# Attention, dense feed-forward and routed experts in one launch: conversions spread out, the opening reordered, scatters and evacuations regrouped

## The chip, the cores and the metric

The kernel runs on one core of a Trainium2 chip. The metric is the device time of one execution in microseconds (us), as the median of several runs. TensorE does the matmuls (PE, with its weight loads as PEld), VectorE is DVE, ScalarE is ACT, GpSimd is POOL, and SyncE (SP) issues most of the DMAs. Each engine works through its own instructions in the order in which the kernel writes them.

## What is computed

The program chains three blocks. The first is bucketed attention over 2 batches x 8 heads, 768 positions, head size 64: a query only sees keys with the same six sign bits of a random projection, and a row without any match falls back on the mean of all values. The second is a dense feed-forward block with a 2048-wide hidden layer and a relu6 gate, on 1536 tokens of width 512. The third routes each token to the best two of eight experts (noisy gate), each expert being a 512-1024-512 block, and adds the two weighted results.

```python
attn = softmax(where(q_bucket == k_bucket, q @ k.T / 8, -1e9)); x = attn @ v
h = x @ w_in;  x = (h * clip(h + 3, 0, 6) / 6) @ w_out
n = x @ w_gate + log1p(exp(x @ w_noise)) * noise
out = sum over the top two e of n:  softmax2(n)[e] * (relu(x @ w1[e]) @ w2[e])
```

The dense weights arrive as 64-bit floats, so the kernel converts them to 32-bit floats on the chip, in 32 halves of a 128x1024 block, and writes them to a scratch tensor `w32` in HBM, from where the dense block loads them.

## The kernel before, in words

**Attention** (line 282 on) runs over 8 pairs of heads (p), each with two halves of the queries (a half of a pair is called hb, 16 in all) and six key tiles, so 96 steps g; a pair is 12 steps (j = 0 to 11). One step does, on TensorE, the four score matmuls of the next step (`scores`, lines 476 and 477; the second of them needs the rows that `stab2` has put into tile A), two matmuls of the running row maximum two halves ahead (`maxes`, line 439, with its reduction on VectorE in line 443), and at every odd g the 48 small matmuls of attention times values for two steps (`av`, line 490). ScalarE makes the exponentials (line 478).

Around it, on GpSimd and VectorE: `stab` (lines 453 to 456, GpSimd) turns the maxima of a finished half into the rows that are transposed and sent into A (`stab2`, lines 464 to 467, the send is a small DMA of ScalarE); `uniform` (line 342, GpSimd) makes the fallback; `finish` (lines 502 to 510) adds it on VectorE, takes the reciprocal and multiplies on GpSimd into `x_all`; `lows` (line 360, GpSimd) makes the low halves of a later pair; `load_v` (line 319) loads the values two pairs ahead, at j = 2, and writes a column of ones on GpSimd (line 320); `v_sum` (lines 326 to 328, GpSimd, five additions, j = 6) sums the values over the key tiles; `bits`, `bits_all` and `move_mask` compute the sign bits and copy them by DMA into the operand tiles A and B.

**The conversion** `conv` (lines 189 to 211) is a generator, resumed once per step by `conv_step`: load 512 KB, wait, two passes on ScalarE (200, 201) and one on VectorE (202), one more on VectorE (205) and an addition on GpSimd (206), then VectorE again (208), then the store. In attention its three tiles come from the pools of the dense weights (three raw buffers `wr`, three high parts `wh`, three low parts `wl`). A conversion starts at every g with g % 3 == 1 until NU = 24 have started; the other eight start at every second step of the dense block. The weights of the first three dense steps are loaded at g = 84 to 86 into the same raw buffers, and split (`w_hi` on ScalarE, `w_lo` on VectorE, line 235) for the first two of them at g = 88 to 91.

**The opening** (lines 525 to 606) prepares the first pair without waiting for the bulk path: constants on VectorE, memsets of the operand tiles on GpSimd, the masks of pair 0 by copies (`mask_q`, line 556, on VectorE) and those of pair 1 by DMA. `bit_consts` (lines 111 to 113), twelve small copies on VectorE, is run with step 0.

**The dense block** takes 48 steps u: three chunks of 512 tokens times 16 hidden tiles, in two passes that are parted at hidden tile FSPLIT = 6. Each step has 12 matmuls into the hidden tile (line 257), activation and split on ScalarE and VectorE, and 12 matmuls into the output (lines 701 to 703). When a chunk is complete, `routing` runs as a generator beside the following steps: transposes, gate, top two, positions (`rt_pos`, lines 807 to 828), and eight indirect scatters of GpSimd into the expert buffers `xg` (`rt_scatter`, line 839). The last chunk's routing runs beside the first expert part, as the table ROUTE says.

**The experts** come in ten parts of eight steps v (`PARTS`); the first two take 224 tokens that the first two chunks filled. `e_load` (line 889) reads a part from `xg`, `e_meta` (898 to 903) its token numbers and weights, `e_out` (973 to 976) scales the result and adds it into the output by an indirect DMA of GpSimd. The part that is loaded third, the first that needs the last chunk's tokens, is loaded through GpSimd's queue.

## Time and profile before

| | us |
|---|---|
| median of 3 runs (917.21 to 921.72) | 918.85 |
| the profiled execution | 919.49 |
| its span, first to last instruction | 917.8 |
| TensorE busy (x6313 matmuls) | 848.0, 92% |
| VectorE, ScalarE, GpSimd busy | 513.6, 423.1, 244.9 |

The span is what the views divide up; 1.7 us of the execution lie outside it. A view of stretches gives each engine's busy time in a stretch, the TensorE clock that was granted there (1.00 is 2.4 GHz, 0.5 is 1.2 GHz, and a mean between says which part of the stretch had which), and the share of the time in which the DMA engines were busy. A matmul's busy time at the lower level is longer, so a busy TensorE is not a fast one. "[7.62 <-DMA V]" behind an instruction means that its engine stood idle for 7.62 us before it and that the named one ended the idle time.

### The profile page before, as it was taken

What the parts mean: (1) busy time and instruction counts of PE and PEld (TensorE: products, weight loads), DVE (VectorE), ACT (ScalarE), POOL (GpSimd) and SP (SyncE); (2) the same over time, 40 slices, a digit from 0 to 9 for tenths busy, and PEclk for the clock granted to TensorE, in tenths of its full rate; (3) what the DMA queues carried; (4) which work ended last, traced back from release to release, by engine and by line L of the source; (5) the groups of instructions that cost most, each with busy time, mean ns of one, the idle gap of its engine ahead of it and who ended that gap; (6) DMA issues with size and microseconds to landing.
All of it is one profiled execution on the core that took longest, in us unless ns stands there. A gap on an engine that the chain in (4) does not pass through costs nothing. (4 is left out here: it accounts for less than half of the span.)

```text
span 917.8 us, 15981 instructions
## 1 busy us (share of the span) xinstructions
PE 848.0 (92%) x6313; PEld 734.3 (80%) x6313; DVE 513.6 (56%) x859; ACT 423.1 (46%) x712; POOL 244.9 (27%) x286
## 2 busy tenths in 40 slices
PE   5889977787899999999999999889999999999993
PEld 2677766676788888888888888769999999999982
DVE  8657856565634666544665566645545445545561
ACT  4356544354555566544444444434433443443551
POOL 9166555274432121100012031521020120202211
PEclk8889998798999999999999999999999999999997
DMA  7655864945603459872225245696465666546671
GB/s 246 164 152 182 262 185 135 260 132 173 190 27 116 160 190 311 281 242 93 92 84 192 70 162 177 209 239 164 140 151 158 144 151 157 136 140 140 177 207 20
DMA packets 52347, 151.74 MB, mean 165 GB/s; under 512 B 8741, under 2 KB 9661, under 8 KB 52265
## 3 DMA queue, kind: packets, MB, share of 16 engines
q1 hardware_dynamic: 44393, 131.02, 46.6%
q0 software_dynamic: 7648, 19.53, 9.4%
q8 instruction: 51, 0.84, 0.4%
q14 instruction: 31, 0.25, 0.1%
q10 hardware_dynamic: 224, 0.10, 0.0%
HBM read 105.89 MB, written 32.41 MB: 151 GB/s over the span
## 5 line engine op out<-in xcount | busy, mean ns | idle before, releaser
L235 DVE TENSOR_TENSOR wl<-wr,wh 128x1024 fp32r<-128x1024 f32 (+1 forms) x128 | 155.9, 1218 | 126.2 <-ACT wh L229 126.2
L229 ACT CAST wh<-wr 128x1024 fp32r<-128x1024 f32 x128 | 134.4, 1050 | 120.0 <-PE S L946 75.8
L478 ACT ACTIVATE E<-S 128x384 f32<-128x384 f32 x192 | 90.5, 490 | 107.6 <-PE S L477 102.4
L976 POOL DMA_INDIRECT out_dram<-ot,ti x28 | 43.8, 1563 | 233.8 <-ACT ot L975 185.4
L443 DVE TENSOR_REDUCE mc<-mx 128x1 f32<-128x768 f32 x96 | 90.6, 951 | 19.7 <-PE mx L439 19.5
L439 PE MATMUL mx<-B,A 128*128 128x384 f32 x192 | 70.9, 383 | 27.3 <-DVE mc L443 24.9
L490 PEld LDWEIGHTS o<-V,E 128*64 128x64 f32 x2304 | 80.0, 151 | 13.8 <-issue 12.2
L273 DVE SCALAR_TENSOR_TENSOR g<-t,mx 128x512 f32<-128x512 f32 x47 | 32.4, 689 | 102.9 <-ACT t L272 102.9
L490 PE MATMUL o<-V,E 128*64 128x66 f32 x2304 | 86.8, 238 | 0.0
L701 PE MATMUL S<-wh,gh 128*128 128x512 f32 (+1 forms) x208 | 82.5, 397 | 0.0
L703 PE MATMUL S<-wh,gl 128*128 128x512 f32 (+1 forms) x208 | 81.6, 392 | 0.0
L702 PE MATMUL S<-wl,gh 128*128 128x512 f32 (+1 forms) x208 | 81.5, 392 | 0.0
L476 PE MATMUL S<-QX,KS 128*128 128x384 f32 x192 | 77.6, 404 | 2.5 <-ACT E L478 2.4
L477 PE MATMUL S<-A,B 128*128 128x384 f32 x192 | 68.8, 358 | 7.3 <-DMA A<-mr 7.3
L944 PE MATMUL S<-hh,wh 128*128 128x416 f32 x192 | 70.6, 368 | 0.0
L945 PE MATMUL S<-hh,wl 128*128 128x416 f32 x192 | 67.5, 352 | 0.0
L946 PE MATMUL S<-hl,wh 128*128 128x416 f32 x192 | 67.4, 351 | 0.0
L439 PEld LDWEIGHTS mx<-B,A 128*128 128x128 f32 x192 | 39.1, 208 | 34.6 <-DVE mc L443 30.6
L925 ACT ACTIVATE hh<-mx 128x416 fp32r<-128x416 f32 (+2 forms) x72 | 33.0, 459 | 65.6 <-PE mx L257 65.6
L272 ACT ACTIVATE t<-mx,half 128x512 f32<-128x512 f32 x47 | 32.3, 688 | 66.2 <-PE mx L257 66.2
L257 PE MATMUL mx<-xh,wh 128*128 128x512 f32 (+1 forms) x252 | 62.2, 369 | 0.6 <-ACT wh L229 0.6
L257 PE MATMUL mx<-xh,wl 128*128 128x512 f32 (+1 forms) x252 | 60.5, 362 | 0.6 <-DVE wl L235 0.6
(246 smaller groups left out, 1640.4 us busy)
## 6 DMA issues: line engine op xcount, KB each, us to landing
wr<-in_we_dram SPq DMA_DIRECT2D x80, 512.0 KB
wr<-w SPq DMA_DIRECT2D x48, 512.0 KB
c_raw<-in_wm_dram SPq DMA_DIRECT2D x32, 512.0 KB
xg<-pt SPq DMA_DIRECT2D x8, 838.5 KB
raw<-in_kq_dram SPq DMA_DIRECT2D x8, 768.0 KB
w<-c_ta SPq DMA_DIRECT2D x24, 256.0 KB
B<-in_kq_dram POOLq DMA_DIRECT2D x7, 768.0 KB, 8.2
xr<-xg SPq DMA_DIRECT2D x5, 838.5 KB
```

Of the source, the lines that this page charges most:

```text
L229: nc.scalar.copy(hi, W[k][0])
L235: nc.vector.tensor_tensor(lo[:, :n], W[k][0][:, :n], W[k][1][:, :n].bitcast(F32), op=ALU.subtract)
L257: nc.tensor.matmul(h, a[:, d * 128:(d + 1) * 128], b[:, d], start=i == 0 and d == 0, stop=i == 2 and d == 3)
L439: nc.tensor.matmul(pm[:, hf, :QW], t["A"][:, qh, q0:q0 + 128], t["B"][:, h, hf * QW:(hf + 1) * QW], start=True, stop=True)
L443: nc.vector.tensor_reduce(t["mc"][:, c:c + 1], pm[:, :, :QW], axis=AX.XY, op=ALU.max)
L476: nc.tensor.matmul(s[:, :QW], t["KS"][:, h, ks], t["QX"][:, qh, qs], start=True, stop=False)
L478: nc.scalar.activation(E[g % NE][:, h], s[:, :QW], ACTF.Exp, scale=0.125)
L490: nc.tensor.matmul(t["av"][r:r + 64, c:c + VW], E[g % NE][:, h, i * 128 + r:i * 128 + r + 64], t["V"][:, kt, h], start=kt == 0 and h == 0 ...
L701: nc.tensor.matmul(o, gh[:, ts], wh, start=first, stop=False)
L702: nc.tensor.matmul(o, gh[:, ts], wl, start=False, stop=False)
L703: nc.tensor.matmul(o, gl[:, ts], wh, start=False, stop=last)
L944: nc.tensor.matmul(o, wh[:, ds], hh, start=ft == 0, stop=False)
```

## The change

Conversions in attention start every sixth step (g % 6 == 3) until 16 have started, instead of every third until 24, and each has two more steps between GpSimd's addition and VectorE's last pass; the other 16 start in three of four dense steps. The ones column is written, and the values summed, at j = 8 instead of j = 2 and 6, and the sum is one reduction of VectorE. GpSimd's product of `finish` moves to the end of the next step. In the opening, `bit_consts` goes to the constants, two pairs of memsets move back and become one each, the second half of pair 0's masks is copied by ScalarE, the first scores come four matmuls into the second half's maxima, and pair 1's mask bits come behind pair 0's maxima, `stab`, `stab2` and `low_q(0)`. FSPLIT becomes 7. The routing generator does its last two transposes in one go and has no pause behind its last scatter; by ROUTE the last chunk's four scatter calls then come together in step v = 3, where the last of them stood behind the part's output scatters. `e_meta(0)` goes from v = 1 to v = 5. The output tiles of the small parts are computed and evacuated one by one.

```diff
-NU = 24
+NU = 16
-ROUTE = [(4, 0, 0), (1, 1, 0), (0, 1, 0), (4, 0, 0)]
+ROUTE = [(3, 0, 0), (1, 1, 0), (0, 1, 0), (5, 0, 0)]
-FSPLIT = 6
+FSPLIT = 7
...
+    bit_consts()
...
         nc.gpsimd.tensor_tensor(t, t, r, op=ALU.add)
-        yield
+        for _ in range(3 if fine else 1):
+            yield
         nc.vector.scalar_tensor_tensor(a, u, 2.0 ** -15, t.bitcast(F32), op0=ALU.is_ge, op1=ALU.mult)
...
-            nc.gpsimd.memset(t["V"][:, :, :, 64:], 1.0)
...
+        def v_sum(p, fill=True):
+            t = T[p]
+            if fill:
+                nc.gpsimd.memset(t["V"][:, :, :, 64:], 1.0)
             vr = sm_p.tile([128, 2 * VW], F32, name="vr")
-            nc.gpsimd.tensor_tensor(vr, V[:, 0], V[:, 1], op=ALU.add)
-            for k in range(2, KT):
-                nc.gpsimd.tensor_tensor(vr, vr, V[:, k], op=ALU.add)
+            nc.vector.tensor_reduce(vr, t["V"].rearrange("p k h c -> p (h c) k"), axis=AX.X, op=ALU.add)
...
-                finish(p, qh, t["av"])
+                at(g + 1, finish(p, qh, t["av"]))
...
-            nc.gpsimd.tensor_tensor(x, ov[:, :, :, 0:64],
-                                    r.unsqueeze(3).to_broadcast([128, 2, KT // 2, 64]), op=ALU.mult)
+            return lambda: nc.gpsimd.tensor_tensor(
+                x, ov[:, :, :, 0:64], r.unsqueeze(3).to_broadcast([128, 2, KT // 2, 64]), op=ALU.mult)
...
-            nc.vector.tensor_copy(A[64:96, hf, h * QW:(h + 1) * QW], mb[64 + 32 * h:96 + 32 * h, hf].bitcast(F32))
+            f = nc.scalar.copy if hf else nc.vector.tensor_copy
+            f(A[64:96, hf, h * QW:(h + 1) * QW], mb[64 + 32 * h:96 + 32 * h, hf].bitcast(F32))
...
-        v_sum(0)
+        nc.gpsimd.memset(T[0]["V"][:, :, :, 64:], 1.0)
+        first_k()
+        mask_q(1, 0)
+        mask_q(1, 1)
+        for i in range(NI):
+            maxes(*more(1, 1)[0])
...
         stab(0)
+        stab2(0)
+        low_q(0)
         for hf in range(2):
             T[1]["pb"] = pbs[hf]
             bits2(1, hf)
             bits3(1, hf)
             lows(1, hf)
...
+        nc.gpsimd.memset(AT[1][64:128].bitcast(F32), 0.0)
+        nc.gpsimd.memset(AT[2][64:128].bitcast(F32), 0.0)
...
-            if i == 5:
+            if i == 3:
+                for _ in scores(0):
+                    pass
+            elif i == 7:
                 low_q(1)
-        for _ in scores(0):
-            pass
+        v_sum(0, False)
...
-            if p + 1 < NP and j == 6:
+            if p + 1 < NP and j == 8:
                 v_sum(p + 1)
-                at(g + 5, v_sum2, p + 1)
+                at(g + 3, v_sum2, p + 1)
...
-                conv_step(1 if g % 3 == 1 and cvn[0] < NU else 0, None, True)
+                conv_step(1 if g % 6 == 3 and cvn[0] < NU else 0, None, True)
...
         for d in range(4):
-            yield rt_trans(c, d)
+            rt_trans(c, d)
+            if d != 2:
+                yield
...
             rt_scatter(c, t)
-            yield
+            if t < 3:
+                yield
...
+            for t in range(nt):
+                gemm2(y, NMU + v, hh, hl, n // nt, ft == 0, ft == 7, (t,))
+                if ft == 7:
+                    e_out(q, t, y[0][:, t, :])
...
-        conv_step(1 - u % 2, cvm_p, False)
+        conv_step(1 if u % 4 < 3 else 0, cvm_p, False)
...
-        if v == 1:
+        if v == 5:
             e_meta(0)
```

## Rows read from the trace of the kernel before

**Rows 1.** Stretches: engines' busy time (instructions), granted clock, DMA share, GB/s; attention by pairs.
```profile
0.00:26.50 26.50, 15.43 (x67) 7.72 (x68) 21.69 (x40) 10.15 (x13) 22.20 (x30) 0.78 0.75 242
26.50:62.20 35.70, 29.56 (x343) 24.46 (x344) 19.68 (x39) 16.11 (x34) 13.06 (x20) 0.83 0.47 128
62.20:88.25 26.05, 25.55 (x380) 21.07 (x376) 20.80 (x31) 16.97 (x37) 16.83 (x30) 1.00 0.78 232
88.25:118.98 30.73, 27.60 (x387) 22.79 (x388) 22.17 (x32) 16.97 (x37) 18.41 (x26) 0.94 0.69 206
118.98:155.48 36.50, 29.52 (x386) 24.29 (x384) 22.27 (x32) 16.86 (x37) 18.34 (x26) 0.86 0.63 191
155.48:193.03 37.55, 29.44 (x386) 24.13 (x384) 22.37 (x32) 16.84 (x37) 18.39 (x26) 0.86 0.63 185
193.03:230.37 37.34, 29.59 (x386) 24.29 (x384) 21.36 (x32) 16.89 (x37) 18.36 (x26) 0.86 0.58 165
230.37:260.00 29.63, 26.89 (x373) 23.24 (x370) 18.93 (x29) 14.45 (x33) 13.44 (x23) 0.94 0.57 166
260.00:286.00 26.00, 25.08 (x404) 20.58 (x402) 7.37 (x12) 13.74 (x30) 5.98 (x8) 1.00 0.12 42
286.00:556.00 270.00, 270.00 (x1242) 222.25 (x1237) 152.78 (x267) 134.43 (x188) 33.63 (x30) 1.00 0.51 170
556.00:626.00 70.00, 63.05 (x393) 53.84 (x392) 44.05 (x106) 32.41 (x57) 19.91 (x16) 0.95 0.71 206
```

**Rows 2.** Waits of TensorE from 62.2 to 260 us: total us, times, longest.
```profile
PE mx L439 <- DVE mc L443: 20.7, 10, 3.3
PE S L477 <- DMA A<-mr: 7.3, 5, 2.5
```

**Rows 3.** Waits of VectorE and of GpSimd in the same stretch.
```profile
DVE c_ta L208 <- POOL c_ta L206: 57.9, 22, 6.6
...
POOL x_all L510 <- DVE r L506: 57.9, 12, 7.2
POOL V L320 <- DMA V<-in_vP_dram: 25.2, 5, 7.6
```

**Rows 4.** Timeline of one stall in pair 4, four engines: start, us, engine, line, what.
```profile
174.42 0.44 PE L477 MATMUL S<-A,B 128*128 128x384 f32 x1 [1.81 <-DMA A<-mr]
...
175.08 0.12 POOL L320 MEMSET V<- 128x24 f32 x1 [7.62 <-DMA V<-in_vP_dram]
...
176.51 0.69 DVE L208 SCALAR_TENSOR_TENSOR c_ta<-c_lu,c_ta 128x512 f32<-128x512 f32 x1 [6.43 <-POOL c_ta L206]
...
178.13 0.69 PE L439 MATMUL mx<-B,A 128*128 128x384 f32 x1 [3.27 <-DVE mc L443]
```

**Rows 5.** Groups of instructions (busy us, mean ns | idle before): GpSimd 62.2 to 260, VectorE to 62.2.
```profile
L206 POOL TENSOR_TENSOR c_ta<-c_ta,c_lu 128x512 int32<-128x512 int32 x22 | 28.0, 1272 | 0.8 <-DVE c_ta L205 0.7
...
L328 POOL TENSOR_TENSOR vr<-vr,V 128x132 f32<-128x132 f32 x24 | 13.1, 545 | 1.9
...
L443 DVE TENSOR_REDUCE mc<-mx 128x1 f32<-128x768 f32 x24 | 22.3, 954 | 15.0 <-PE mx L439 14.9
L556 DVE CAST A<-mb 32x384 fp32r<-32x384 f32 x4 | 3.8, 947 | 0.1
```

**Rows 6.** Timeline of the opening and of the first pair.
```profile
25.44 1.74 SPq L126 DMA_DIRECT2D A<-mb  x2
...
32.07 0.66 PE L439 MATMUL mx<-B,A 128*128 128x384 f32 x1 [2.37 <-DMA A<-mb]
...
50.40 0.38 PE L464 MATMUL z<-ident,nr 128*12 128x128 f32 x1 [3.46 <-POOL nr L455]
```

**Rows 7.** Timeline of VectorE near the end of attention: the split at g = 89.
```profile
274.60 1.23 DVE L235 TENSOR_TENSOR wl<-wr,wh 128x1024 fp32r<-128x1024 f32 x1
```

**Rows 8.** Waits of TensorE from 556 to 626 us.
```profile
PE S L807 <- DVE r_cc L798: 2.8, 1, 2.8
PE mx L914 <- DMA xr<-xg: 2.7, 1, 2.7
```

**Rows 9.** Timeline of the end: the first evacuation of the last part.
```profile
902.33 0.68 ACT L975 ACTIVATE ot<-S,w 96x512 f32<-96x512 f32 x1 [2.44 <-PE S L703]
```

More of the change, by code (lines that the diff above doesn't have):

```diff
@@ L531, in first @@
             nc.gpsimd.memset(B[96:128].bitcast(F32), 0.0)
-            for i in range(1, 3):
-                nc.gpsimd.memset(AT[i][96:128].bitcast(F32), 0.0)
-                nc.gpsimd.memset(AT[i][64:96].bitcast(F32), 0.0)
             nc.vector.tensor_copy(A[0:64, 0], raw[64:128, 0])
@@ L579, in chain_kernel @@
             pbs.append(T[1]["pb"])
-        first_k()
-        for i in range(NI):
-            maxes(*more(1, 1)[0])
-        mask_q(1, 0)
-        mask_q(1, 1)
         stab(0)
+        stab2(0)
+        low_q(0)
         for hf in range(2):
@@ L590, in chain_kernel @@
             lows(1, hf)
-            if hf == 0:
-                stab2(0)
-                low_q(0)
+        nc.gpsimd.memset(AT[1][64:128].bitcast(F32), 0.0)
+        nc.gpsimd.memset(AT[2][64:128].bitcast(F32), 0.0)
         with tc.issue_after(T[0]["nrd"].ins):
@@ L599, in chain_kernel @@
             maxes(*more(1, 2)[0])
-            if i == 5:
+            if i == 3:
+                for _ in scores(0):
+                    pass
+            elif i == 7:
                 low_q(1)
-        for _ in scores(0):
-            pass
+        v_sum(0, False)
         at(0, v_sum2, 0)
-        at(0, bit_consts)
         pend = []
@@ L694, in chain_kernel, with gemm2 @@
     cvm_p = mctx.enter_context(tc.tile_pool(name="cvm", bufs=2, reuse_waits="tile"))
-    def gemm2(y, k, gh, gl, m, first, last, nt=4):
+    def gemm2(y, k, gh, gl, m, first, last, ts=range(4)):
         wh, wl = W[k][1][:, 512:], W[k][2][:, 512:]
-        for t in range(nt):
+        for t in ts:
             o = y[t // 2][:m, t % 2, :]
-            ts = slice(t * m, (t + 1) * m)
-            nc.tensor.matmul(o, gh[:, ts], wh, start=first, stop=False)
-            nc.tensor.matmul(o, gh[:, ts], wl, start=False, stop=False)
-            nc.tensor.matmul(o, gl[:, ts], wh, start=False, stop=last)
+            c = slice(t * m, (t + 1) * m)
+            nc.tensor.matmul(o, gh[:, c], wh, start=first, stop=False)
+            nc.tensor.matmul(o, gh[:, c], wl, start=False, stop=False)
+            nc.tensor.matmul(o, gl[:, c], wh, start=False, stop=last)
     def m1_second(u):
@@ L937, in m2_second @@
         if not sw:
-            gemm2(y, NMU + v, hh, hl, n // nt, ft == 0, ft == 7, nt)
+            if ft == 7:
+                ex["o", q] = e_tile(q, [128, 4, 512], "ot", "xh")
+                ex["st", q] = []
+            for t in range(nt):
+                gemm2(y, NMU + v, hh, hl, n // nt, ft == 0, ft == 7, (t,))
+                if ft == 7:
+                    e_out(q, t, y[0][:, t, :])
         else:
@@ L947, in m2_second @@
         W.pop(NMU + v)
-        if ft == 7:
+        if ft == 7 and sw:
             ex["o", q] = e_tile(q, [128, 4, 512], "ot", "xh")
             ex["st", q] = []
-            if not sw:
-                for t in range(nt):
-                    e_out(q, t, y[0][:, t, :])
-            else:
-                yt = ex["yt", q] = e_tile(q, [128, 4, CAP], "yt", bufs=1)
-                for d in range(4):
-                    f = (nc.scalar.copy, nc.vector.tensor_copy)[d % 2]
-                    f(yt[:, d, :n], y[d // 2][:, d % 2, :n])
+            yt = ex["yt", q] = e_tile(q, [128, 4, CAP], "yt", bufs=1)
+            for d in range(4):
+                f = (nc.scalar.copy, nc.vector.tensor_copy)[d % 2]
+                f(yt[:, d, :n], y[d // 2][:, d % 2, :n])
     def e_back(q, t):
@@ L1033, in chain_kernel @@
         route(kb)
-        if v == 1:
+        if v == 5:
             e_meta(0)
-        elif v == 3:
+        if v == 3:
             e_meta(1)
```

2 lines of the change are left out of this document (removed).

## The prediction

> **What bounds the kernel now.** I read the stretches first [rows 1]. From 286 us on TensorE is busy without a gap up to the last expert part, except in the 70 us from 556, where 7 us are missing. So in the dense and expert blocks only what TensorE does counts, and other engines' work is free there as long as it fits. Attention is different. Its pairs do the same work (some 385 matmuls), yet pair 1 takes 26.05 us, with TensorE busy for 25.55 of them, and pairs 3 to 5 take 36.50 to 37.55. There the granted clock is 0.86, so 0.28 of the time was spent at the lower level: after each long wait TensorE runs slowly for a while, which the busy column hides. Pair 1 is therefore what a pair costs when nothing makes TensorE wait, and the six pairs 1 to 6 cost 26.05 + 30.73 + 36.50 + 37.55 + 37.34 + 29.63 = 197.8 us against 6 x 26.05 = 156.3. The excess is 41.5 us, and all of it is waiting or its aftermath.
>
> The waits name it [rows 2]: 20.7 us in ten waits for the reduction of VectorE (line 443) and 7.3 us in five for the small transfer of `stab2`. VectorE in turn waited 57.9 us, 22 times, for GpSimd's addition of the conversion, and GpSimd waited 57.9 us for the reciprocal of `finish` and 25.2 us for values still in flight [rows 3]. One stall shows the chain whole [rows 4]: GpSimd stands for 7.62 us at the ones column, because the values have not landed; its addition comes next in its queue; VectorE stands for 6.43 us at line 208 for that addition; the maxima's reduction comes next in VectorE's queue; TensorE stands 3.27 us for that. No engine is full: in pair 4 VectorE is busy for 22.37 of 37.55 us and GpSimd for 18.39 [rows 1]. Queue order is the bound.
>
> **The change part by part.**
>
> Pairs 1 to 6. The ones column moves six steps behind its load's issue, so the 25.2 us of GpSimd's waiting go. The product of `finish` stands at the end of the next step, behind the next `stab`, so GpSimd no longer stops 57.9 us for a reciprocal with `stab` and the addition queued behind it [rows 3]. Line 208 comes three steps after the addition instead of one; a step of pair 1 is 26.05 / 12 = 2.2 us [rows 1], so VectorE asks some 4.3 us later, and the addition takes 1.27 us [rows 5]. Four of the five additions of the value sum alone were 4 x 0.545 = 2.2 us of GpSimd per pair, between two `lows` for whose result the mask transfers wait; they go, and VectorE gets one reduction of 792 elements, priced by that of 768: 0.954 x 792 / 768 = 0.98 us [rows 5]. Two conversions per pair instead of four take half of these passes away. What is late next? The transfer of `stab2`: five waits, 7.3 us [rows 2], 1.5 us each. Its place in the order does not change, but the burst of large transfers around it loses one of two conversion loads, and `stab` no longer stands behind `finish`. I keep 1 us a pair for it: 6 x 27.05 = 162.3, a gain of 35.5 us. Bounds: 41.5, if every pair is like pair 1; and if one stall a pair is left, as in pair 2, pairs 3 to 5 fall to 30.73 and the gain is 5.8 + 6.8 + 6.6 = 19 us.
>
> This 1 us is where a rule can be weighed. The row says that the small transfer, issued on ScalarE's own queue, ended five waits of up to 2.5 us. The Trainium skill (DMA: Bandwidth & Descriptors, "Queues, rings and completion order") says that each DMA engine takes turns between the queue rows that have work, packet by packet, by which a small transfer on a row of its own should hardly wait for another row's large ones. By that rule the residue would be nil, the gain 41.5 and the time 870; the trace does not agree, so the residue stays.
>
> The opening and pair 0, together 62.2 us. TensorE waits at 32.07 for pair 1's masks in A, which SP sent from 25.44 on [rows 6]. The mask bits move ahead: two copies of `mask_q` leave VectorE for ScalarE (2 x 0.947 us [rows 5]), four memsets of GpSimd are no longer ahead of `stab`, `bit_consts` runs while VectorE has nothing to do at the start. I take 3 us, between the 1.9 of the copies alone and 4.3, copies and the whole wait of 2.37. Later, at 50.40, TensorE waits 3.46 us for `stab` on GpSimd [rows 6], whose queue has the product of `finish` ahead of it; the product moves, the wait goes, and with it the slow stretch behind it. Pair 0 takes 35.70 us at a clock of 0.83, 9.65 more than pair 1 [rows 1]; I take half of that, 5. Sum 8, bounds 2 and 14. No queue gets a new wait here that I see; the moved memsets have `lows` ahead of them and pair 2's operands behind them, which are wanted a pair later.
>
> The last steps of attention lose. Conversions now start at g = 87 and 93. The one of 87 needs a raw buffer, and all three then hold dense weights; the first comes free when `w_lo` of g = 89 has ended, at 274.60 + 1.23 = 275.8 [rows 7]. Its load starts only then, but ScalarE's pass over it stands in the order at g = 90, ahead of the next exponentials, and the scores have two banks. The nearest rows for a transfer's latency are the waits for landings, 1.8 to 7.6 us [rows 4]. The DMA engines are nearly idle there (share 0.12 [rows 1]), so I take 4 us for ScalarE and TensorE behind it, and 1 more for the conversion of 93, which is flushed in one go ahead of the third weights' split. Sum +5, bounds 0 and 8.
>
> The dense block. Eight conversions more run there: each has three passes on VectorE and two on ScalarE over 512 columns, at most 5 x 0.954 (768 columns [rows 5]), so 8 x 2.9 = 23 us on VectorE and 15 on ScalarE, beside 117 and 136 idle us [rows 1]; GpSimd adds 8 x 1.27. The cover is TensorE's 270 us, and a step's product is wanted a step later, so nothing, with up to 4 us if loads collide. FSPLIT moves chunk borders, not work.
>
> From 556 to 626. TensorE waits 2.75 us for the top two (line 798) and 2.7 for the expert tokens [rows 8]. `e_meta(0)`, on VectorE ahead of the first, goes: half, 1.4 us. The last scatter call moves ahead of the output scatters, and the load behind it starts earlier: 2.7 us. The clock of 0.95 costs 0.05 x 70 = 3.5 us; a third comes back, 1. The DMA engines are busy there (0.71 [rows 1]), and the earlier tokens' load meets the weights: 1 us back. Sum 4, bounds -1 and 7.
>
> The end. ScalarE's first evacuation starts after the part's last matmul [rows 9] though its own tile is done three matmuls before; evacuated singly it starts earlier, by no more than its own 0.68 us: 0.7.
>
> **Sum.** 35.5 + 8 - 5 + 0 + 4 + 0.7 = 43.2 us off the profiled execution's 919.49: 876.3. The median is 0.6 lower: 876.
>
> **The rivals.**
>
> A new wait takes the place of half the old ones. GpSimd keeps its two `lows` and the product of `finish` in the same two steps, and the small transfer may wait longer once the steps are shorter. For it: pair 2 had no wait at the ones column and still took 30.73. Against: pair 1, with four conversions, took 26.05. Gain 19 + 8 - 5 + 4 + 0.7 = 26.7, time 892. Chance 0.2.
>
> The reduction on VectorE lands on the path. Seven of them at 0.98 us in front of the maxima's reductions would give back 6.9 us: 883. Against: VectorE is idle for 5.2 of pair 1's 26.05 us and loses six conversion passes a pair. Chance 0.08. The Trainium skill (VectorE: DVE Perf Modes, "Rules for kernel authors") calls this reduction the slowest operation of the engine and advises to restructure rather than put one on a hot path, which speaks against this edit; no run here shows this one yet.
>
> The edits miss the cause: the DMA engines' traffic sets the pairs (share 0.58 to 0.63 in pairs 3 to 5), and order changes little. Against: pair 1 ran with 0.78 [rows 1]. Then only the opening's small end, the routing and the end pay against the 5 us: 919.5 - 2 - 4 - 0.7 + 5 = 918. Chance 0.04.
>
> Slower: in the dense block the conversions' loads, three in four steps, queue behind the weights and the zero fills, and ScalarE, waiting for one ahead of its activations, stops TensorE in each of 21 steps. To cancel 43 us it has to cost 2.1 us a step; at 2.5, the longest wait seen for the small transfer [rows 2], it costs 52.5 and gives 929. Against: eight conversions ran there without a gap [rows 1]. Chance 0.03.
>
> **How the numbers follow.** The forecast has the remaining 0.65. Its own range is 862 to 890. Taking the first rival in, I give 860 to 896; the bounds of all terms together would reach 856 and 911. What a measurement can tell is 0.5%, 4.6 us. Faster by more: 0.93; within: 0.04; slower: 0.03.
>
> **What would show it.** Right: pairs 1 to 6 within 26 to 28 us at a clock near 1.00; line 208 hardly waiting; no wait at the ones column; pair 1 starting near 54; one wait of ScalarE for a conversion's load near the end of attention; the tokens' load before TensorE wants it. Wrong, if pairs stay above 30 us, if the dense block exceeds 270 us by more than a few, or if VectorE's waits for GpSimd only change their line.

## The result and the profile after

The changed kernel takes 883.55 us (median of 4, 878.66 to 884.83), the kernel before 918.80 (median of 4, 917.21 to 921.72). The ratio is 0.9607, 95% interval 0.9569 to 0.9646: 35 us faster, 7.5 us short of the 876 that were forecast, and inside the range. The profiled execution of the changed kernel was its fastest, 878.66 us with a span of 876.8; so stage by stage the traces explain 41 us.

The stages can be cut at the same work in both traces: at the first exponential of a pair, the third and the last activation of the dense block, and the first, 17th and last of the experts. These are the two profiled executions, in us:

| stage | before | after | gain |
|---|---|---|---|
| to pair 1 (opening, pair 0) | 62.2 | 50.8 | 11.4 |
| pairs 1 to 6 | 197.8 | 160.7 | 37.1 |
| pair 7 to the third dense step | 35.1 | 43.4 | -8.3 |
| to the last dense step | 258.6 | 260.5 | -1.9 |
| to the first expert step | 7.6 | 8.7 | -1.1 |
| 16 expert steps (routing beside them) | 61.7 | 56.8 | 4.9 |
| the other expert steps | 276.6 | 278.5 | -1.9 |
| to the end of the span | 18.2 | 17.4 | 0.8 |

The view of stretches of the changed kernel, cut so (columns: time and length, then the busy us and instructions of PE, PEld, DVE, ACT, POOL, the granted clock, the DMA share, GB/s):

```profile
0.00:19.75 19.75, 14.21 (x63) 5.81 (x64) 15.74 (x47) 11.26 (x16) 12.48 (x19) 0.91 0.81 265
19.75:50.81 31.06, 26.76 (x338) 21.68 (x336) 21.27 (x24) 13.75 (x31) 13.24 (x19) 0.95 0.55 151
50.81:77.43 26.62, 25.59 (x380) 21.23 (x380) 20.46 (x29) 14.39 (x33) 13.07 (x25) 1.00 0.70 192
...
131.28:157.92 26.64, 25.49 (x380) 21.17 (x380) 20.58 (x28) 14.42 (x32) 11.95 (x18) 1.00 0.72 206
...
211.47:254.90 43.43, 36.47 (x441) 29.10 (x440) 18.83 (x29) 21.32 (x42) 10.68 (x12) 0.92 0.32 101
254.90:515.40 260.50, 259.46 (x1188) 213.20 (x1187) 159.56 (x281) 137.47 (x198) 41.61 (x37) 1.00 0.58 195
...
524.10:580.90 56.80, 51.80 (x344) 44.18 (x343) 36.86 (x96) 27.73 (x49) 19.76 (x15) 1.00 0.73 214
```

Against [rows 1], every pair now takes 26.6 to 27.2 us at a clock of 1.00, so the excess of 41.5 us over six times pair 1 is down to 4.4. The stretch that lost most is the end of attention, at 0.92. The waits of the changed kernel from 50.81 to 211.47 us (engine, line, waited for: total us, times, longest), with all of TensorE's:

```profile
DVE vr L329 <- POOL V L327: 7.9, 6, 1.5
PE mx L440 <- DVE mc L444: 7.2, 6, 1.7
...
PE S L477 <- ACT E L479: 0.2, 1, 0.2
```

Of the waits of [rows 2] and [rows 3] one kind is left, once a pair, at its start. There is no wait for the small transfer into A, none of VectorE for the conversion's addition, none of GpSimd for the values; GpSimd's for the reciprocal is down from 57.9 to 0.8 us (it now stands 68.1 us, in twelve waits for the maxima, ahead of `stab`). The timeline of the changed kernel there (start, us, engine, line, what) shows its chain:

```profile
76.48 0.12 POOL L327 MEMSET V<- 128x24 f32 x1
...
76.63 1.58 DVE L329 TENSOR_REDUCE vr<-V 128x132 f32<-128x792 f32 x1 [1.45 <-POOL V L327]
...
78.13 1.81 DVE L444 TENSOR_REDUCE mc<-mx 128x1 f32<-128x768 f32 x2
79.13 0.19 PEld L440 LDWEIGHTS mx<-B,A 128*128 128x128 f32 x1 [2.06 <-DVE mc L444]
79.13 0.44 PE L440 MATMUL mx<-B,A 128*128 128x384 f32 x1 [1.74 <-DVE mc L444]
```

GpSimd comes late to the ones column, VectorE stands for it in front of the new value sum, the sum takes 1.58 us, and the maxima's reduction that TensorE needs is behind it in VectorE's queue. At the end of attention the timeline of the changed kernel is:

```profile
227.29 5.23 SPq L191 DMA_DIRECT2D c_raw<-in_wm_dram  x2
...
230.91 0.69 ACT L202 ACTIVATE c_lu<-c_raw 128x512 int32<-128x512 uint32 x1 [4.45 <-DMA c_raw<-in_wm_dram]
...
233.53 0.69 PE L477 MATMUL S<-QX,KS 128*128 128x384 f32 x1 [4.85 <-ACT E L479]
```

The load of the conversion of g = 87 is issued as soon as its raw buffer comes free, at 227.29; ScalarE stands for it until 230.91 ahead of the exponentials, and TensorE for 4.85 us. Its next matmul takes 0.69 us, at the lower clock.

In the routing's stretch TensorE no longer waits for `xr`, and for the top two 1.5 instead of 2.75 us [rows 8]. The singly evacuated output tiles brought a wait that had not been there. Timeline of the changed kernel at the end of the ninth part:

```profile
840.17 0.68 ACT L981 ACTIVATE ot<-S,w 96x512 f32<-96x512 f32 x1 [0.36 <-PE S L704]
840.90 0.16 PEld L702 LDWEIGHTS S<-wh,hh 128*96 128x96 f32 x1 [1.24 <-ACT ot L981]
840.91 0.47 PE L702 MATMUL S<-wh,hh 128*96 128x512 f32 x1 [0.77 <-ACT ot L981]
```

Both tiles are halves of one buffer `y`; TensorE begins the second at 840.91, when ScalarE has read the first (until 840.85). That comes once in each of the four small parts: 1.08, 0.78, 0.77 and 0.77 us.

### The profile page after: what moved, and what is told of

Same layout as the page of the kernel before. It is cut to its first block, busy times and chain, and to the rows that moved or that the text cites. A ratio compares the mean times of both kernels' runs of the same rounds, so it can differ in the third digit from the quotient of the medians.

```text
span 876.8 us, 15979 instructions
## 1 busy us (share of the span) xinstructions
PE 829.8 (95%) x6313; PEld 717.1 (82%) x6313; DVE 524.4 (60%) x865; ACT 422.2 (48%) x714; POOL 214.5 (24%) x244
## 4 chain that ended last, share of the span: by engine, by line
PE 79%; DVE 8%; DMA 3%; issue 3%; ACT 3%; POOL 2%; POOLq 0%; ACTq 0%; SPq 0%; DVEq 0%
PE mx L260 28%; PE o L491 7%; PE S L702 5%; PE S L704 5%; PE S L703 5%; PE S L954 4%; PE S L955 4%; PE S L956 4%; PE S L477 4%; PE mx L440 3%; PE S L478 3%; DVE mc L444 2%; DVE wl L238 1%; DVE vr L329 1%; ACT wh L232 1%
## 5 line engine op out<-in xcount | busy, mean ns | idle before, releaser
L491 PEld LDWEIGHTS o<-V,E 128*64 128x64 f32 x2304 | 72.7, 140 | 12.3 <-issue 9.6
L477 PE MATMUL S<-QX,KS 128*128 128x384 f32 x192 | 75.7, 394 | 6.2 <-ACT E L479 6.0
L491 PE MATMUL o<-V,E 128*64 128x66 f32 x2304 | 79.4, 226 | 0.0
L440 PE MATMUL mx<-B,A 128*128 128x384 f32 x192 | 64.6, 349 | 11.8 <-DVE mc L444 9.3
L478 PE MATMUL S<-A,B 128*128 128x384 f32 x192 | 65.6, 342 | 1.4 <-DMA A<-mr 1.4
L260 PE MATMUL mx<-xl,wh 128*128 128x512 f32 (+1 forms) x252 | 60.2, 360 | 0.0
```

The costliest lines, as they stand in the source:

```text
L260: nc.tensor.matmul(h, a[:, d * 128:(d + 1) * 128], b[:, d], start=i == 0 and d == 0, stop=i == 2 and d == 3)
L477: nc.tensor.matmul(s[:, :QW], t["KS"][:, h, ks], t["QX"][:, qh, qs], start=True, stop=False)
L491: nc.tensor.matmul(t["av"][r:r + 64, c:c + VW], E[g % NE][:, h, i * 128 + r:i * 128 + r + 64], t["V"][:, kt, h], start=kt == 0 and h == 0 ...
```

## The experiments

Each was one kernel, compared with the kernel before in the same session. "After" stands for the changed kernel with one edit, "before" for the kernel before with one part of the change.

**1. After, conversions closer, so that the last starts earlier.**

```diff
-g % 6 == 3 and cvn[0] < NU
+g % 5 == 3 and cvn[0] < NU
```

> The changed kernel with its 16 conversions of attention five steps apart, so that the last starts at g = 78, ahead of the weights' loads. Theory: the last pair and the first dense step lost some 8 us because the conversion of g = 87 had to wait for a raw buffer and ScalarE, in order, stood behind its load (4.45 us) and behind the last conversion (4.35 us). With the buffers free again both waits go, the last pair takes 25 to 26 us, pairs 1 to 6 stay at 26.6 to 27.3, and the time falls by 7 to 9 us against the changed kernel's 878.7 to 884.8. Rival: the waits only cover others, such as the third weights' load, which comes late in any case; then less than 2 us are gained. Second rival: conversions five steps apart bring the pairs' stalls back, and the pairs go above 28 us.

Measured: 876.79 us (873.14 to 879.73), ratio 0.9562 [0.9538, 0.9587]. Pair 7 to the third dense step fell from 43.4 to 34.7 us, and the waits for `c_raw` and the weights went. But two pairs became longer; stretches of this kernel, pairs 2 and 4 with pair 3 between them:

```profile
77.25:107.12 29.87, 27.10 (x380) 22.70 (x380) 24.18 (x33) 14.89 (x32) 13.04 (x19) 0.94 0.70 196
107.12:133.57 26.45, 25.48 (x380) 21.18 (x380) 18.76 (x27) 15.66 (x35) 12.58 (x19) 1.00 0.78 216
133.57:162.12 28.55, 27.16 (x382) 23.01 (x383) 21.34 (x32) 14.85 (x34) 12.15 (x18) 0.94 0.68 192
```

At the start of these two pairs VectorE stood 3.1 and 3.2 us for the ones column (1.45 in the changed kernel), in the first of them a conversion's pass (line 211) followed the sum ahead of the maxima, TensorE's wait grew to 2.68 and 2.16 us, and the clock fell behind it. In the changed kernel, with six steps, no conversion's pass stands at that place. The late conversions are what the end of attention lost to.

**2. After, with the spacing undone:** 24 conversions, every third step, the addition read one step later, every second dense step.

```diff
-NU = 16
+NU = 24
...
-g % 6 == 3
+g % 3 == 1
...
-        for _ in range(3 if fine else 1):
-            yield
+        yield
...
-conv_step(1 if u % 4 < 3 else 0, cvm_p, False)
+conv_step(1 - u % 2, cvm_p, False)
```

> The changed kernel with the conversions as before: 24 in attention, every third step, one step between the addition and VectorE's last pass, eight in the dense block. Theory of queue order: what made the pairs slow was GpSimd standing at the ones column and at the product of finish with the addition queued behind; both stay mended here, so the pairs stay below 28.5 us, the wait near the end of attention goes because the last conversion starts at g = 70, and the time is 870 to 880 us. Rival, density: the gain came from having half the conversions and more steps between addition and last pass; then pairs 3 to 5 go back above 31 us and the time is above 895.

Measured: 900.61 us (891.63 to 902.03), 0.9786 [0.9729, 0.9842]. Pairs 1 to 6 took 181.6 us, 21 more than with the spacing. Waits of this kernel from 61.2 to 242.8 us:

```profile
PE mx L439 <- DVE mc L443: 12.2, 4, 3.1
PE S L477 <- DMA A<-mr: 2.8, 3, 1.5
...
DVE vr L328 <- POOL V L326: 12.5, 5, 2.5
DVE c_ta L210 <- POOL c_ta L208: 10.4, 18, 0.6
```

The order of the queues alone (ones column, sum, `finish`) holds 16.2 us of the gain in the pairs, not 37.1. At five pair starts VectorE stands 2.5 us for the ones column, and a conversion's pass (line 207) follows the sum ahead of the maxima; TensorE's wait there is 3.0 us in the mean, against 1.2.

**3. Before, with the ones column and the value sum as changed, and nothing else.**

```diff
         def load_v(p):
...
-            nc.gpsimd.memset(t["V"][:, :, :, 64:], 1.0)
...
         def v_sum(p):
...
+            nc.gpsimd.memset(t["V"][:, :, :, 64:], 1.0)
...
-            nc.gpsimd.tensor_tensor(vr, V[:, 0], V[:, 1], op=ALU.add)
-            for k in range(2, KT):
-                nc.gpsimd.tensor_tensor(vr, vr, V[:, k], op=ALU.add)
+            nc.vector.tensor_reduce(vr, t["V"].rearrange("p k h c -> p (h c) k"), axis=AX.X, op=ALU.add)
...
-            if p + 1 < NP and j == 6:
+            if p + 1 < NP and j == 8:
```

> The kernel before with the ones column and the value sum changed alone: both at j = 8, the sum by one reduction on VectorE. Theory of queue order: the stall in the middle of pairs 3 to 5 goes (7.6 us of GpSimd at the ones column, 3.3 us of TensorE and the slow clock behind), the wait for the maxima at a pair's start stays in part, so pairs 3 to 5 take 30 to 32 us and the time is 895 to 905. Density: no more than 5 us are gained, since conversions are as dense as before.

Measured: 902.01 us (900.60 to 904.12), 0.9829 [0.981, 0.9849]. Pairs 1 to 6: 179.5 us, 18.3 less than before; VectorE's wait for the addition fell from 57.9 to 17.8 us, its longest from 6.6 to 1.1. TensorE's waits for the maxima that are left stand at the pairs' starts; those in the middle of a pair, of which [rows 4] shows one, are gone. So the stand at the ones column, at which GpSimd had nothing else to do, was the head of that chain. How the 18.3 us divide between the column and the sum, which went from GpSimd to VectorE in the same edit, was not tried.

**4. Before, with the product of `finish` moved, and nothing else.**

```diff
-                finish(p, qh, t["av"])
+                at(g + 1, finish(p, qh, t["av"]))
```

> The kernel before with the product of finish moved to the end of the next step alone. Theory of queue order: GpSimd no longer stands 57.9 us for the reciprocal, but it still stands at the ones column, so the stall in the middle of a pair stays; the first pair loses its wait of 3.5 us, and the time is 905 to 916. Rival: this wait was the whole cause, since stab and the addition stood behind it, and the pairs go to 27 us and the time below 890. Rival the other way: idle GpSimd time there cost nothing, and the time stays within 3 us of before.

Measured: 921.43 us (7 runs, 917.48 to 923.61), 1.0024 [1.0004, 1.0045]; pairs 1 to 6 199.8 us. Waits of this kernel from 62.4 to 262.2 us:

```profile
POOL c_ta L206 <- ACT E L478: 55.2, 10, 7.9
DVE c_ta L208 <- POOL c_ta L206: 54.9, 21, 6.5
...
POOL V L320 <- DMA V<-in_vP_dram: 25.2, 5, 7.7
PE mx L439 <- DVE mc L443: 22.3, 9, 3.7
```

GpSimd no longer waits for the reciprocal, but it waits as long at the next instruction of its queue, and VectorE's and TensorE's waits are what they were. In this kernel those 57.9 us were spare time of GpSimd, not a cause; what the move is worth beside the other edits was not tried. In the opening TensorE's wait for `stab`, which the prediction put down to the product [rows 6], was still there, at 50.27 us with 2.96 us.

**5. Before, with the spacing alone**, in attention and in the dense block.

```diff
-NU = 24
+NU = 16
...
-g % 3 == 1
+g % 6 == 3
...
-        yield
+        for _ in range(3 if fine else 1):
+            yield
...
-conv_step(1 - u % 2, cvm_p, False)
+conv_step(1 if u % 4 < 3 else 0, cvm_p, False)
```

> The kernel before with the conversions of the change alone: 16 in attention, every sixth step, three steps between the addition and VectorE's last pass, 16 in the dense block. The ones column still stands on GpSimd behind its load at j = 2 and the sum is still GpSimd's. Density: an addition late on GpSimd no longer reaches VectorE, because its last pass comes three steps later, so the pairs go to 26.5 to 28 us, the last pair loses its 8 us to the raw buffer, and the time is 888 to 897. Queue order: GpSimd's stand of 7.6 us at the ones column still holds the addition past three steps, pairs 3 to 5 stay above 31 us, and the time is above 903.

Measured: 904.12 us (900.11 to 907.97), 0.9824 [0.9786, 0.9861]. Pair 1 started at 55.6 us, 6.6 earlier than before; pairs 1 to 6 took 182.3, 15.5 less. Waits of this kernel from 55.6 to 237.9 us, and its timeline round one of them:

```profile
POOL V L321 <- DMA V<-in_vP_dram: 43.9, 5, 10.7
...
PE S L478 <- DMA A<-mr: 20.9, 6, 4.8
...
DVE c_ta L209 <- POOL c_ta L206: 3.8, 5, 1.1
```

```profile
94.11 0.62 ACTq L468 DMA_DIRECT2D A<-mr  x1
...
102.73 0.69 PE L478 MATMUL S<-A,B 128*128 128x384 f32 x1 [3.95 <-DMA A<-mr]
```

The spacing takes VectorE's wait for GpSimd away by itself, but the 6 KB of `stab2` now come late: issued by 94.73, there at 102.73. The DMA engines' share from 94 to 103 us, in 40 slices of this stretch (9 is 90% or more), was

```profile
DMA  9997979998999996999699997999999999999976
```

with loads of 768 KB issued at 87.86 and 92.67 us and the values at 90.96. The dense block with eight conversions more, but the old routing, took 258.2 us, 0.3 less than before: they cost nothing there. The end of attention, with the late conversions, took 44.2 us against 35.1 here too.

**6. After, with both tiles computed before either is evacuated**, as before the change.

```diff
-            for t in range(nt):
-                gemm2(y, NMU + v, hh, hl, n // nt, ft == 0, ft == 7, (t,))
-                if ft == 7:
-                    e_out(q, t, y[0][:, t, :])
+            gemm2(y, NMU + v, hh, hl, n // nt, ft == 0, ft == 7, range(nt))
+            if ft == 7:
+                for t in range(nt):
+                    e_out(q, t, y[0][:, t, :])
```

> The changed kernel with both output tiles of a small part computed before either is evacuated, as before. Theory: computed singly, the second tile's matmuls wait for ScalarE's evacuation of the first (1.1, 0.8, 0.8 and 0.8 us in the four parts), and only the last part earns something, by an earlier scatter; so three of the waits are pure loss, and joint is 1 to 2.5 us faster than the changed kernel. Rival: what the prediction said, singly is a gain of 0.7 us at the end and nothing elsewhere; then joint is 0.7 slower.

Measured: 880.54 us (878.90 to 882.17), 0.9577 [0.9548, 0.9605]. The 16 expert steps took 55.4 us against 56.8, the others 276.5 against 278.5, the end 17.9 against 17.4; no wait for ScalarE at the parts' ends is left. The 2.0 us of the later steps are firm: all seven traces with single evacuation in every small part took 278.5 to 278.7 us there, the seven others 276.5 or 276.6. The 1.4 us of the 16 steps are not, since with single evacuation this stage took 55.4 to 57.2 us from trace to trace; the wait itself is 1.08 us there. The medians show 3.0 us in sum, with intervals that overlap.

**7. After, with the ones column on VectorE, right ahead of the sum.**

```diff
-                nc.gpsimd.memset(t["V"][:, :, :, 64:], 1.0)
+                nc.vector.memset(t["V"][:, :, :, 64:], 1.0)
```

> The changed kernel with the ones column written by VectorE instead of GpSimd, just ahead of the reduction. Theory: once a pair TensorE waits 0.9 to 1.7 us for VectorE's maxima, because VectorE stands 1.4 us for GpSimd's ones column and then needs 1.58 us for the sum of the values; without the stand the wait falls below 0.5 us, pairs 1 to 6 go from 26.6 to 27.3 to 26.1 to 26.3, and the time falls by 2 to 6 us. Rival: the reduction's own 1.58 us is what TensorE waits for, and the wait stays above 0.8 us and the time within 2 us.

Measured: 885.34 us (884.47 to 887.90), 0.9631 [0.9608, 0.9654]: no gain. Of TensorE's waits from 55.3 to 215.3 us the one for the maxima is gone, and another has its place:

```profile
PE S L478 <- DMA A<-mr: 6.4, 6, 1.9
```

6.4 us in six waits against 7.2 in six: the small transfer was next in line, and TensorE's stand at the pair's start had covered it.

**8. After, with the value sum back on GpSimd**, at its new place j = 8.

```diff
-            nc.vector.tensor_reduce(vr, t["V"].rearrange("p k h c -> p (h c) k"), axis=AX.X, op=ALU.add)
+            V = t["V"].rearrange("p k h c -> p k (h c)")
+            nc.gpsimd.tensor_tensor(vr, V[:, 0], V[:, 1], op=ALU.add)
+            for k in range(2, KT):
+                nc.gpsimd.tensor_tensor(vr, vr, V[:, k], op=ALU.add)
```

> The changed kernel with the value sum on GpSimd again, five additions at j = 8 behind the ones column. Theory that the reduction on VectorE is what costs a pair its 1.2 us: TensorE's wait for the maxima goes, but GpSimd, which reaches the ones column only near j = 10, then needs 3 us for the sum, and TensorE waits in its place for the sum's matmul at j = 11: 0 to 2 us a pair slower, the time within 0 to 10 us above the changed kernel. Rival, GpSimd has room since it stands for nothing else: pairs at 26.1 us and the time 2 to 6 us lower.

Measured: 881.79 us (878.58 to 883.11), 0.96 [0.9574, 0.9626]. Pairs 1 to 6 took 158.7 us; the waits for the maxima are gone, those for the small transfer are 4.0 us in four. Pairs 4 to 6 took 25.2 to 25.5 us, less than the 26.05 that the prediction took as what a pair costs. Pair 3 took 29.6 us at a clock of 0.94; the longest of these waits, 1.6 us, stands in it. The overall difference to the changed kernel is too small for these runs.

**9. After, with 14 conversions in attention**, so that the last starts at g = 81, ahead of the weights, at the distance of six.

```diff
-NU = 16
+NU = 14
```

> Question: is the loss at the end of attention due to the two conversions that start behind the weights' loads (g = 87 and 93)? Here 14 start in attention, the last at g = 81, at the same distance of six steps, and 18 in the dense block. Theory (the late conversions wait for a raw buffer and stop ScalarE and TensorE): the waits of 4.45 us of ScalarE for c_raw, 4.85 us of TensorE and 1.44 us for wh go, the way from pair 7's first exponential to the third dense activation falls from 43.4 to about 36 us, pairs 1 to 6 stay at 26.6 to 27.3 us, time 873 to 877. Rival 1 (the splits of the dense weights themselves take that place, with or without conversions): the way stays above 41 us, time 881 to 885. Rival 2 (two more conversions overload the dense block): the way falls, but the dense activations 3 to 48 take 265 us and more instead of 260.5, time 880 and more.

Measured: 875.46 us (871.39 to 880.63), 0.9519 [0.9474, 0.9564], 8.1 us below the changed kernel. Stretches of this kernel, end of attention and dense block:

```profile
219.23:253.80 34.57, 33.65 (x440) 27.58 (x440) 14.41 (x23) 18.85 (x37) 9.07 (x10) 1.00 0.33 108
253.80:514.30 260.50, 259.45 (x1188) 213.15 (x1188) 162.82 (x287) 139.56 (x201) 44.22 (x39) 1.00 0.59 198
```

43.4 us became 34.6, at a full clock, and the dense block did not become longer with two conversions more. The loss at the end of attention is those two late conversions, 8.8 us. This execution started pair 1 only at 57.1: TensorE waited 6.4 us there for the masks (below, in the last section).

**10. Changed kernel with the old opening.** Its order, the sign-bit constants, the mask copies and the memsets as before; the rest as changed.

```diff
...
-        first_k()
-        mask_q(1, 0)
-        mask_q(1, 1)
-        for i in range(NI):
-            maxes(*more(1, 1)[0])
         pbs = []
         for hf in range(2):
             bits(1, hf)
             pbs.append(T[1]["pb"])
+        first_k()
+        for i in range(NI):
+            maxes(*more(1, 1)[0])
+        mask_q(1, 0)
+        mask_q(1, 1)
         stab(0)
...
```

> Question: what is the new opening worth by itself? The changed kernel with the old order of the opening (sign-bit constants at step 0, both halves of the masks copied by VectorE, pair 1's bits ahead of the maxima, first scores last, four memsets ahead of stab). Theory (the order of the opening gives about what pair 1's earlier start shows, 62.2 to 50.8 us): pair 1 starts at 58 to 62 us, pairs 1 to 6 unchanged at 26.6 to 27.3 us, time 890 to 894. Rival (much of the earlier start came from the spacing of the conversions and from finish, as pair 0 has two conversions less): pair 1 starts at 52 to 55 us, time 884 to 888.

Measured: 881.32 us (880.30 to 888.81), 0.9621 [0.9563, 0.968], level with the changed kernel. Pair 1 started at 52.3 us, against 50.8. Stretches of this kernel, opening and pair 0:

```profile
0.00:24.75 24.75, 15.59 (x67) 7.66 (x68) 20.60 (x40) 10.16 (x13) 19.95 (x24) 0.82 0.83 259
24.75:52.31 27.56, 26.06 (x333) 21.18 (x332) 20.46 (x34) 13.85 (x31) 9.23 (x15) 0.92 0.51 131
```

The new order brings the first exponential 5 us forward (19.75 instead of 24.75) and gives 3.5 of them back in pair 0, where TensorE now waits 1.75 us for the value sum of VectorE (at 24.91) and 1.30 ahead of pair 1's first maxima (at 27.06). The theory of the expectation fell. Of the 9.9 us by which pair 1 starts earlier here than in the kernel before, the spacing alone gave 6.6 (experiment 5); where the others come from was not tried. The 1.5 us between 52.3 and 50.8 are less than what this start differs by from trace to trace (last section).

**11. Before, with the routing's regrouping alone:** the new table, the two merged pauses, `e_meta(0)` at v = 5.

```diff
-ROUTE = [(4, 0, 0), (1, 1, 0), (0, 1, 0), (4, 0, 0)]
+ROUTE = [(3, 0, 0), (1, 1, 0), (0, 1, 0), (5, 0, 0)]
...
-        if v == 1:
+        if v == 5:
             e_meta(0)
```

> Question: what is the routing's regrouping worth by itself? The kernel before with the new routing table, the two merged pauses of the routing, and the token numbers' load at v = 5 instead of 1; nothing else. Theory (the scatters in one row let the third part's tokens arrive in time): TensorE's wait of 2.7 us for xr goes, the one for the top two falls to about 1.5 us, the way from the first expert activation to the seventeenth falls from 61.7 to about 57 us, time 913 to 916, ratio 0.994 to 0.997. Rival (FSPLIT and the earlier dense block gave that): waits as before, time 918 to 920.

Measured: 915.77 us (10 runs, 913.53 to 917.68), 0.9972 [0.9954, 0.999]. The 16 expert steps took 56.6 us against 61.7, and of [rows 8] one wait is gone and one halved, in the waits of this kernel from 556 to 626 us:

```profile
PE S L807 <- DVE r_cc L798: 1.5, 1, 1.5
```

5.1 us gained there, 1.4 lost in the dense block (258.6 to 260.0). There TensorE waits twice 0.52 us for the split of a weight on VectorE (line 235), which it does not in the kernel before; that the merged pauses, which put more of the routing into one step, make VectorE late is an inference.

**12. A version of the parts that the runs bear out:** the changed kernel with 14 conversions, the sum on GpSimd, and single evacuation only in the last part. (The sum's edit is that of experiment 8.)

```diff
-NU = 16
+NU = 14
...
+            single = q + 1 == len(PARTS)
+            for ts in [(t,) for t in range(nt)] if single else [range(nt)]:
+                gemm2(y, NMU + v, hh, hl, n // nt, ft == 0, ft == 7, ts)
...
```

> The parts that the runs so far bear out, together: 14 conversions in attention, the value sum on GpSimd at j = 8, and output tiles computed together before they are evacuated except in the last part. Theory: the gains add up, as they lie in different stretches: about 7 to 8 us at the end of attention, 2 to 3 us at the three earlier evacuations (no wait of TensorE for ScalarE at the ends of the small parts), 1 to 3 us at the pair starts; time 868 to 873, 3 to 6 us below the run with 14 conversions alone. Rival: the stalls of the small transfer in tile A come back in place of the value sum's, so that it stands level with the run with 14 conversions alone.

Measured: 864.25 us (863.27 to 866.61), 0.9414 [0.9374, 0.9455]: 19 us below the changed kernel, and more than its parts promised. Stretches of this kernel, pairs 1 to 6 and the end of attention:

```profile
51.48:207.93 156.45, 152.66 (x2278) 128.35 (x2277) 115.28 (x160) 87.42 (x194) 85.52 (x144) 1.00 0.68 188
207.93:242.50 34.57, 33.64 (x440) 27.59 (x440) 14.33 (x23) 18.83 (x37) 9.06 (x10) 1.00 0.34 108
```

Against the profiled execution of the changed kernel (876.8 to 862.9 us of span) 4.2 us come from the pairs, 8.8 from the end of attention and 2.0 from the later expert steps; 1.6 were lost ahead of pair 1 and in the 16 expert steps. The other 5 us of the medians' difference are not in these two traces; the changed kernel's profiled execution was 5 us below its median.

## Why the prediction was right, and where it was not

**Pairs 1 to 6** were forecast at 162.3 us, a gain of 35.5, and took 160.7. The reading of [rows 4], ones column to addition to reduction, was right: parting its links by spacing alone gave 15.5 us (experiment 5), by the ones column and the sum alone 18.3 (3), and the whole change 37.1. But it is one stall of two. The other stands at each pair's start, and there GpSimd does not wait but works. GpSimd, VectorE and TensorE of the kernel before at the start of pair 4:

```profile
151.43 0.65 POOL L326 TENSOR_TENSOR vr<-V 128x132 f32<-128x132 f32 x1
152.16 2.48 POOL L328 TENSOR_TENSOR vr<-vr,V 128x132 f32<-128x132 f32 x4
154.60 1.83 POOL L360 TENSOR_TENSOR KS<-raw,B 128x768 fp32r<-128x768 f32 x1
...
157.20 1.26 POOL L206 TENSOR_TENSOR c_ta<-c_ta,c_lu 128x512 int32<-128x512 int32 x1
...
158.49 0.69 DVE L208 SCALAR_TENSOR_TENSOR c_ta<-c_lu,c_ta 128x512 f32<-128x512 f32 x1 [4.41 <-POOL c_ta L206]
...
160.11 0.44 PE L439 MATMUL mx<-B,A 128*128 128x384 f32 x1 [2.44 <-DVE mc L443]
```

The value sum (3.1 us) and `lows` stand ahead of the conversion's addition without a gap; VectorE waits 4.41 us for that addition, and TensorE 2.44. Five such waits, 2.2 to 2.4 us each, are 12 of the 20.7 us in [rows 2]. The edits that the prediction priced take this stall apart too, since the sum leaves GpSimd and line 208 comes later, but it names the ones column alone as the head. It also misread pair 2, which did wait at the ones column, for 2.56 us at 102.72 (and pair 1 for 1.10); what slowed pair 2 was mostly the stall at its start, 2.23 us.

One of the three causes named was none: GpSimd's 57.9 us before the product of `finish` were called a stop for the work behind it, and moving the product gained nothing (4). The step that failed took an engine's idle time for a delay; nobody waited for what stood behind it any longer than before.

**The residue** of 1 us a pair was of the right size (1.2 us were waited, and a pair takes 0.7 more than pair 1 before), but the wrong cause was named. The prediction kept the small transfer of `stab2`; in the changed kernel no pair waits for it. The mis-sized term was the value sum on VectorE: 0.98 us, from a reduction of 768 elements to one [rows 5]. This one, of 792 elements to 132, took 1.58 (1.60 in the mean), and the prediction did not cost the wait for the ones column ahead of it, up to 1.45. So the second rival came true in mechanism: the sum stands in front of the maxima. That the measured 883.55 us is also that rival's time is chance: the pairs gave 1.6 us more than forecast, and what is missing lies elsewhere. The Trainium skill (VectorE: DVE Perf Modes, "Rules for kernel authors") calls this operation the engine's slowest and advises to consider restructuring where it is on a hot path; the trace agrees, since with the sum on GpSimd the wait is gone (8). The transfer is the next limit behind it, as 7 and 8 showed with 6.4 and 4.0 us. By the rule of the Trainium skill weighed in the prediction (DMA: Bandwidth & Descriptors, "Queues, rings and completion order") each DMA engine takes turns between the queue rows packet by packet. What the prediction drew from it, that a small transfer on a row of its own hardly waits, is not what the trace shows: in experiment 5 it took 8 us beside bulk loads.

**The opening and pair 0** gave 11.4 us in the two traces where 8 were forecast, mostly for a reason that was not in the sum. With the spacing alone pair 1 started 6.6 us earlier (5), and with the old order the changed kernel's time is level (10): no run shows a gain of the mask copies and the constants, for which 3 us were taken. The 11.4 are also the lucky end: in the seven traces with this opening and 14 or 16 conversions in attention (the changed kernel, 1, 6, 7, 8, 9 and 12) pair 1 started at 50.8 to 57.1 us, 5 to 11 us earlier than before. The 5 us put down to the product of `finish` failed too: with the product moved, the wait for `stab` remained (4), and with the spacing alone it was down to 1.72.

**The end of attention** lost 8.3 us where 5 were forecast. The mechanism was right in each link: raw buffer, late load, ScalarE ahead of the exponentials, TensorE. ScalarE stood for 4.45 us and TensorE for 4.85, near the 4 taken. The conversion of g = 93 was put at 1: ScalarE stood 4.35 us for its last pass ahead of the third weights' split, and TensorE 1.44 for that split. What was left out is the clock behind the first wait: it was at 0.50 from 231.6 to 238.4, and the 4.9 us that TensorE worked from 233.5 on are by that about 2.4 us more than at 1.00. The three make 8.7 us (an estimate from these rows); experiment 9 gave 8.8 back.

**The dense block** was put at 0 to 4 us and lost 1.9: not the eight conversions (5: none), but mostly the routing's regrouping (11: 1.4). The further 1.1 us before the first expert part appear in every kernel with FSPLIT 7 (8.5 to 11.5 us against 7.6 with 6): there TensorE waits 0.7 to 2.1 us for the first part's tokens, and with 6 in no trace. The prediction put FSPLIT at nothing, as it moves borders and not work; that edit was not tried alone.

**The routing's stretch** was forecast at 4 and gave 4.9; by itself 5.1 (11). **The end** gave 0.5 to 0.8, as forecast. What was missed is that the same edit works at the ends of the three other small parts: it was costed at its last place alone, and lost 2.0 us at two of the others and, by its wait, about 1 us at the third (6).

**The sum** came to 43 us forecast and 41 in the traces, and that it is so near is in part luck: the gains came out some 6 us larger than forecast (3.4 of them in the opening), against some 8 us of losses that were forecast too small or not at all. The median of the changed kernel lies 5 us above its profiled execution, and of that the prediction had nothing.

## What to carry to other kernels

When several engines' queues stall in a ring, find the head of each stall (here a one-eighth-microsecond memset waiting for a load in the middle of a pair, and a backlog of GpSimd's own work at its start) and give each link more steps; a long idle time of an engine counts only if somebody behind it is waited for. Before work is started at regular places, look at the last places, where its buffers have another owner: two late conversions cost a fifth of what the whole change gained. When a loop body is changed for the sake of its last iteration, cost it in every iteration, and write it for the last one alone.

## What the runs showed of the hardware that had not been expected

**Two engines at the same memory.** In pairs 1 to 6 the conversion's pass on VectorE that reads two tensors in SBUF (line 207) took 0.68 us in seven of twelve cases and 2.24 or 2.25 in the other five, each time when GpSimd's `lows` (line 361) had started about 0.14 us before it. Timeline of the changed kernel:

```profile
71.92 1.84 POOL L361 TENSOR_TENSOR KS<-raw,B 128x768 fp32r<-128x768 f32 x1
...
72.06 2.25 DVE L207 SCALAR_TENSOR_TENSOR c_ta<-c_raw,c_ta 128x512 int32<-128x512 int32 x1
...
85.27 0.68 DVE L207 SCALAR_TENSOR_TENSOR c_ta<-c_raw,c_ta 128x512 int32<-128x512 int32 x1
```

2.25 is 1.57 us more than alone, about what `lows` still had to run (1.70). In pair 0 it started with 0.90 us of `lows` to run, and took 1.45. By the Trainium skill (SBUF — State Buffer, "Summary: rules for kernel authors") the second of two such instructions stands until the first has ended; the trace agrees.

**A small transfer's arrival differs from execution to execution.** In the opening, pair 1's masks go by small DMAs of SyncE, 42 KB each. In the profiled execution of the changed kernel they had landed when TensorE began pair 1's maxima at 27.06 us, at most 2.6 us after their issue at 22.76 to 24.50 (the profile puts the 1.30 us of waiting before that down to GpSimd). In that of experiment 9, with the same opening, issued at 23.83 to 25.58, they came at 32.38. Timelines of the two:

```profile
22.76 1.74 SPq L128 DMA_DIRECT2D A<-mb  x2
...
27.06 0.66 PE L440 MATMUL mx<-B,A 128*128 128x384 f32 x1 [1.30 <-POOL ng L454]
```

```profile
23.83 1.75 SPq L128 DMA_DIRECT2D A<-mb  x2
...
32.38 0.66 PE L440 MATMUL mx<-B,A 128*128 128x384 f32 x1 [6.40 <-DMA A<-mb]
```

The profiled executions of experiments 2, 6 and 7 had this wait too (4.5 to 5.2 us), that of 8 a shorter one for the masks in B (1.96), those of 1 and 12 none. With the old opening TensorE comes later (29.96 us in experiment 10), and no wait there is put down to the masks. This would explain why the changed kernel's runs lie between 878.7 and 884.8 us; with one trace a kernel it is not shown.
